# Filter placement by 32-column array tiles, x in half loads, and turns moved ahead of the rounds, in an FFT mixing and FFN kernel

## The chip, the cores and the metric

The kernel runs on one NeuronCore of a Trainium2 chip. The metric is the device time of one execution in microseconds, the median over several runs; times inside the kernel are from one profiled execution, counted from the start of its span (755.9 us).

## The reference

For each of 8 batches, x (3008 x 256) is filtered along the sequence by an FFT, a product with a complex filter and an inverse FFT. The result, as 24064 rows of 256, goes through an FFN with a squared ReLU.

```python
X = np.fft.rfft(x, axis=1)
Y = X * (filt_r + 1j * filt_i)[None, :, :]
y = np.fft.irfft(Y, n=x.shape[1], axis=1)        # 8 x 3008 x 256
h = np.maximum(y.reshape(24064, 256) @ w_in, 0)  # w_in 256 x 2048
out = (h * h) @ w_out                            # w_out 2048 x 256
```

## The kernel before

The length 3008 is split as 64 x 47, and the transforms are matmuls with constant matrices. A batch passes through five stages:

- stage A, 47-point transforms of x; batch 0 has a form of its own (`chunk_a0`, L375 and L377, evicted to `uT` by ScalarE in L384 and VectorE in L386) because it comes first and nothing else can run yet;
- the turn: batch 0's result is transposed on TensorE by an identity (`turn_u`, L394, evicted to `ut` in L400 and L402); later batches go through DRAM;
- stage B (`unit_b`, L417) and the product with the filter on VectorE (L425), which writes `prods`;
- stage P (`unit_p0`, L448), evicted by ScalarE to `ze` (L450), written to DRAM and read back in another layout as `zt`;
- stage Y (`unit_y`, L498), which gives `yt`, the input of the FFN (`ffn_g1`, L528, with the ReLU in L532).

The filter reaches its place by matmuls too. Its 1504 rows are loaded flat on 128 partitions (L237), cast to 16 bits, and moved by `place_f`: for each of 24 channels, a matmul with a 0/1 matrix picks the rows of the lower half (L284), a second one those of the upper half and adds them (L287). Both matrices are 128 x 128 and write all 128 output partitions, because each of 4 groups of 32 partitions holds one of the two halves (`low, up, low, up`). ScalarE evicts the result to `sF` (L295), the imaginary part with a sign by partition. `place_f(im, k)` covers four channels; there are six for the real and six for the imaginary part.

The order is written out by hand, and each engine runs its instructions in that order. Before the planned main loop there is a prologue for batch 0: the three loads of x, 1 MB each (`load_wide`, L215), then the filters and constants on the same queue; 26 warm-up matmuls on zeros (L265); five halves of x cast by VectorE and one by GpSimd (L219); stage A in four chunks; turns 0 to 3; a real placement; the casts of the imaginary filter; turn 4, a real placement, turn 5, an imaginary placement; then seven rounds. A round runs two `unit_b`, an imaginary placement between them, a `unit_p0` of the round before and a real placement. After the rounds come batch 1's stage A (L348), fill matmuls that keep TensorE busy (L799), stage Y of batch 0, and the loop over the FFN, into which the later batches' stages are planned by due times.

PSUM has three kinds of pairs: `psH` (two tiles of two banks), `psF` and `psO` (two of one bank each). `bank_pair` hands them out in turn: psH, psH, the psF pair, the psO pair. In the rounds placements and `unit_p0` share the two psH tiles, so each waits for the eviction of the one before the last.

Of the kernel before, what the change touches and what calls it, by code (L numbers as in the profile page):

```python
# [9 lines left out]
F16 = mybir.dt.float16  # L10
# [10 lines left out]
SLOTS = 8  # L21
CLS = 376
QF = 3008
PQ = ((0, 0), (0, 1), (0, 2), (1, 2), (1, 3), (1, 0))


def _build_consts():
    N = N1 * N2
    n2 = np.arange(N2)
    m = np.arange(NM)  # L30


    SA = np.zeros((N2, 2, 2, 2, NC))
    for c in range(NC):
        for h in range(2):
            SA[:, h, h, 0, c] = np.cos(2 * np.pi * n2 * c / N2)
            SA[:, h, h, 1, c] = np.sin(2 * np.pi * n2 * c / N2)

    S0 = np.zeros((128, 6, 2, 48))
    for h in range(2):
        q = SA[:, h, h].reshape(N2, 48)
        for t in range(2):
            S0[2 * h + t::4, t, h] = q[:32]
        for c in range(4):
            S0[4 * h + c:120:8, 2 + c, h] = q[32:]


    freq = np.full((NC, 64), -1)  # L50
    for c in range(NC):
        for j in range(32):
            freq[c, j] = 47 * j + c
            if c:
                freq[c, 32 + j] = 47 * j + 47 - c
    freq[0, 32] = N // 2


    SB = np.zeros((NM, 2, 2, NC, 2, 64))

    n1j = 8 * (m % 8) + 2 * (m // 8)
    SP = np.zeros((2, 64, NC, 2, 2, NM))
    for c in range(NC):
        for f in range(64):
            k = freq[c, f]
            if k < 0:
                continue
            sg = 1.0 if (f < 32 or c == 0) else -1.0
            for h in range(2):
                th = 2 * np.pi * ((k * (32 * h + m)) % N) / N  # L70
                SB[:, h, 0, c, 0, f] = np.cos(th)
                SB[:, h, 1, c, 0, f] = -sg * np.sin(th)
                SB[:, h, 0, c, 1, f] = -np.sin(th)
                SB[:, h, 1, c, 1, f] = -sg * np.cos(th)
            if c == 0 and f == 32:
                SB[:, :, 1, c, :, f] = 0.0
            w = (1.0 if k in (0, N // 2) else 2.0) / N
            for i in range(2):
                th = 2 * np.pi * ((k * (n1j + i)) % N) / N
                cs, sn = w * np.cos(th), w * np.sin(th)  # L80
                SP[0, f, c, i, 0] = cs
                SP[0, f, c, i, 1] = sg * sn
                SP[1, f, c, i, 0] = -sn
                SP[1, f, c, i, 1] = sg * cs


    SY = np.zeros((32, 2, 2, N2, 2))
    for c in range(NC):
        th = 2 * np.pi * c * n2 / N2
        for i in range(2):  # L90
            SY[c + c // 12 * 4, i, 0, :, i] = np.cos(th)
            SY[c + c // 12 * 4, i, 1, :, i] = -np.sin(th)


    PF = np.zeros((128, 6, 2, 2, 32))
    for w, (s, q) in enumerate(PQ):
        for j in range(32):
            PF[4 * j + q, w, :, s, j] = 1.0

    f16 = lambda a, p: np.ascontiguousarray(a.reshape(p, -1).astype(np.float16))  # L100
    C0 = np.zeros((128, 896))
    C0[:, 0:576] = S0.reshape(128, 6, 2, 2, NC).transpose(0, 1, 4, 2, 3).reshape(128, 576)
    C0[:, 576:704] = np.eye(128)
    for h in range(2):
        C0[64 * h:64 * h + N2, 704:752] = SA[:, h, h].reshape(N2, 48)
    C0[:, 768:862] = SY.reshape(128, 94)
    return f16(C0, 128), f16(PF, 128), f16(SB, 128), f16(SP, 128)


@with_exitstack  # L110
def kernel(
# [90 lines left out]
    sSA = sC1[:, 0:64]  # L202
    sSY = sC1[0:112, 64:158]
    ident = sC0[:, 576:704]
    sPF = p_out.tile([128, 6, 128], F16, tag="ost", name="sPF")

    xw32, xw16 = {}, {}

    def load_wide(k):

        v0 = xrows[0:2048, :].rearrange("(p m) d -> p m d", m=16)
        v1 = xrows[2048:3072, :].rearrange("(p m) d -> p m d", m=8)
        pool, tag = (p_x32, "x32") if k < 2 else (p_h2, "h2")
        t = pool.tile([128, 8, D], F32, tag=tag, name=f"xw_{k}")
        nc.sync.dma_start(out=t, in_=(v0[:, 0:8, :], v1, v0[:, 8:16, :])[k])  # L215
        xw32[k] = t

    def cast(eng, out, in_):
        (eng.copy if eng is nc.scalar else eng.tensor_copy)(out=out, in_=in_)  # L219

    def cast_wide(k, *engs):
        t = p_x16.tile([128, 8, D], F16, tag="x16", name=f"xw16_{k}")
        for i in range(2):
            m = slice(4 * i, 4 * i + 4)
            cast(engs[i], t[:, m, :], xw32[k][:, m, :])
        xw16[k] = t

    for k in range(3):
        load_wide(k)


    f32s = []

# [5 lines left out]
        f32s.append(t)  # L239

    load_f(0)
    nc.sync.dma_start(out=sPF, in_=dPF.ap().rearrange("p (w q) -> p w q", q=128))
    load_f(1)
    nc.sync.dma_start(out=sC1, in_=dC0.ap()[:, 704:896])
    nyq = p_out.tile([128, 2, D], F32, tag="ost", name="nyq")
# [15 lines left out]
    sF = const.tile([128, 2, NC, D], F16, name="sF")  # L261
    nc.vector.memset(sF[:, 0, 0:2, :], 0.0)
    ps = psO("warm").rearrange("p a d -> p (a d)")
    for _ in range(26):
        nc.tensor.matmul(ps, zero, sF[:, 0, 0:2, :], start=True, stop=True)  # L265

    f16s = []
# [1 line left out]
    def place_f(im, k, *engs, rotate=False):  # L269
# [6 lines left out]
        for i in range(4):  # L276
            c = 4 * k + i
            e0, e1 = D * c, D * (47 - c)
            cuts = [0] + [d for d in range(1, D)
                          if (e0 + d) % QF == 0 or (c and (e1 + d) % QF == 0)] + [D]  # L280
            for d0, d1 in zip(cuts, cuts[1:]):
                o = banks[i // 2][:, (i % 2) * D + d0:(i % 2) * D + d1]
                q, a = divmod(e0 + d0, QF)
                nc.tensor.matmul(o, sPF[:, PQ.index((0, q)), :], f16s[0][:, im, a:a + d1 - d0],  # L284
                                 start=True, stop=False)
                q, a = divmod(e1 + d0, QF) if c else (0, QF + d0)
                nc.tensor.matmul(o, sPF[:, PQ.index((1, q)), :], f16s[0][:, im, a:a + d1 - d0],  # L287
                                 start=False, stop=True)
        for t, i in groups:
            n = t.shape[1]  # L290
            eng = engs[i % len(engs)]
# [71 lines left out]
        if b == 1:  # L363
            write_u(b, c)

    def chunk_a0(c):

        for k in range(2):
            banks, groups = bank_pair(f"psA_0_{c}_{k}")
            for dt in range(2):  # L370
                for i in range(4):
                    m = 4 * k + i
                    o = banks[dt][:, 96 * i:96 * i + 96]
                    d = slice(128 * dt, 128 * dt + 128)
                    nc.tensor.matmul(o, xw16[2 * (c % 2)][:, m, d], s0[:, c // 2, :],  # L375
                                     start=True, stop=False)
                    nc.tensor.matmul(o, xw16[1][0:120, m, d], s0[0:120, 2 + c, :],  # L377
                                     start=False, stop=True)
            for dt in range(2):
                m = 32 * c + 16 * k  # L380
                o = uT[:, dt, :, m:m + 16].rearrange("p c (m q) -> p m c q", q=4)
                pv = banks[dt][:, 0:384].rearrange("p (m c q) -> p m c q", m=4, q=4)
                if (pair_engine() is nc.scalar) if len(groups) == 1 else (dt == 0):
                    nc.scalar.copy(out=o, in_=pv)  # L384
                else:
                    nc.vector.tensor_copy(out=o, in_=pv)  # L386

    def turn_u(k, eng):

# [343 lines left out]


    uT = p_h2.tile([128, 2, NC, 128], F16, tag="h2", name="uT")
    for k in range(3):
        cast_wide(k, nc.vector, nc.gpsimd if k == 2 else nc.vector)

    def load_const(t, d, k):
        c = slice(12 * k, 12 * k + 12)  # L740
        nc.sync.dma_start(out=t, in_=d.ap().rearrange("p (a b) -> p a b", b=128)[:, c, :])
# [3 lines left out]
        load_const(sSB[:, c, :], dSB, k)  # L745
        load_const(sSP[:, c, :], dSP, k)
    load_win()
    for c in (0, 2, 1, 3):
        chunk_a0(c)
    f16s.append(p_h2.tile([128, 2, QF + D], F16, tag="h2", name="f16"))  # L750
    e0, e1 = slice(0, 1504), slice(1504, QF)
    for im in range(2):
        nc.gpsimd.tensor_copy(out=f16s[0][:, im, QF:], in_=nyq[:, im, :])
    for e in (e0, e1):
        nc.gpsimd.tensor_copy(out=f16s[0][:, 0, e], in_=f32s[0][:, e])
    uts[0] = p_ut.tile([128, NC, D], F16, tag="ut", name="ut_0")
    turn_u(0, nc.scalar)
    turn_u(1, nc.vector)
    turn_u(2, nc.scalar)
    turn_u(3, nc.vector)  # L760
    place_f(0, 0, nc.scalar, rotate=True)
    for eng, e in ((nc.vector, slice(0, 1024)), (nc.gpsimd, slice(1024, 2048)),
                   (nc.scalar, slice(2048, QF))):
        cast(eng, f16s[0][:, 1, e], f32s[1][:, e])
    turn_u(4, nc.vector)
    place_f(0, 1, nc.scalar, rotate=True)
    turn_u(5, nc.vector)
    place_f(1, 0, nc.scalar, nc.vector, rotate=True)
    for k in range(6):
        if k % 3 == 0:  # L770
# [9 lines left out]
    for k in range(7):  # L780
        if k < 6:
            unit_b(0, 2 * k)
            if k < 5:
                place_f(1, k + 1, nc.scalar)
            unit_b(0, 2 * k + 1)
        if k > 0:
            unit_p0(k - 1)
        if k < 4:
            place_f(0, k + 2, nc.scalar)
    read_z(0, 0)  # L790
    read_z(0, 1)
    tiny = const.tile([1, 1], F16, name="tiny")
# [67 lines left out]
```

## Time and profile before

The median of three runs is 759.61 us (759.55 to 760.27).

| engine | busy us | share of the span |
|---|---|---|
| TensorE matmul | 741.9 | 98% |
| VectorE | 655.4 | 87% |
| ScalarE | 564.2 | 75% |
| GpSimd | 193.9 | 26% |

The change concerns the time before the first FFN matmul, at 50.21 us:

| event | us |
|---|---|
| first cast of x starts | 6.32 |
| stage A, first matmul | 11.23 |
| turns without a further wait from | 17.80 |
| first product with the filter starts | 24.62 |
| last `ze` copy starts | 41.24 |
| stage Y starts | 48.76 |
| first FFN matmul starts | 50.21 |

A row of a timeline gives start, length, engine, line, operation, output and inputs, count, and in brackets how long the engine was idle before and what ended that. Matmul lengths include their latency, so the spacing of starts says more than the length of one. A row of "groups" gives busy time and mean length; idle time there counts only where the engine is the one that the end waits for.

### The profile page before, as it was taken

The page shows a single profiled execution, that of the slowest core. Times are in us where ns is not written, and L with a number is a line of the kernel's source. Part 1 is how long each engine was busy: PE and PEld are TensorE (multiplying, and loading weights), DVE is VectorE, ACT ScalarE, POOL GpSimd, SP SyncE. Part 2 cuts the span into 40 slices and gives each one's busy share as a digit, 9 for nine tenths or more (in the row PEclk, how much of TensorE's full clock was granted, in tenths as well). Part 3 has the DMA queues.
Part 4 walks back from the last instruction along what each step waited for, and adds up shares of the span by engine and source line. Part 5 has one row for each costly group of instructions (what it writes and reads, how often), then busy time and mean ns, then how long its engine had stood idle before and what let it go on. Part 6 is the DMA issues. An engine that isn't in the chain of part 4 may idle for free.

```text
span 755.9 us, 20010 instructions
## 1 busy us (share of the span) xinstructions
PE 741.9 (98%) x8419; PEld 542.8 (72%) x8419; DVE 655.4 (87%) x730; ACT 564.2 (75%) x803; POOL 193.9 (26%) x267
## 2 busy tenths in 40 slices
PE   8988999999999999999999999999999999999998
PEld 5845766777777777877778777787678777777776
DVE  5859998899899898989979998899989989888783
ACT  2967788778878777787777778777777777777773
POOL 3811750244222321232303224033311222000000
PEclk9999999999999999999999999999999999999999
DMA  9994898666785566756586646764547333321011
GB/s 364 298 221 147 144 185 224 174 115 121 165 220 121 97 130 161 194 104 133 107 216 127 131 102 131 229 126 101 115 108 207 80 78 92 99 85 43 30 57 57
DMA packets 103026, 106.51 MB, mean 141 GB/s; under 512 B 10144, under 2 KB 93472, under 8 KB 101400
## 3 DMA queue, kind: packets, MB, share of 16 engines
q1 hardware_dynamic: 83496, 81.99, 35.7%
q0 software_dynamic: 19296, 23.05, 22.1%
q8 instruction: 66, 1.08, 0.6%
q14 instruction: 24, 0.20, 0.1%
q10 hardware_dynamic: 144, 0.18, 0.1%
HBM read 57.97 MB, written 48.23 MB: 141 GB/s over the span
## 4 chain that ended last, share of the span: by engine, by line
PE 90%; DVE 5%; ACT 2%; DMA 1%; issue 1%; ACTq 0%; DVEq 0%
PE psH L528 40%; PE psX L643 21%; PE psY L643 16%; PE psY L498 3%; PE psB L417 2%; PE psP L462 2%; PE psA L348 2%; DVE prod L425 2%; PE warm L265 1%; PE psO L548 1%; ACT h L532 1%; DVE h L539 1%; PE psf L284 1%; PE psf L287 1%; DMA prod<-prod 1%
## 5 line engine op out<-in xcount | busy, mean ns | idle before, releaser
L532 ACT ACTIVATE h<-psH 128x1024 f16<-128x1024 f32 x376 | 385.3, 1026 | 160.2 <-PE psH L528 159.2
L528 PE MATMUL psH<-yt,sWin 128*128 128x512 f16 (+7 forms) x1728 | 386.8, 351 | 1.2 <-ACT h L532 0.4
L539 DVE TENSOR_TENSOR h<-h 128x2048 f16<-128x2048 f16 (+1 forms) x192 | 229.8, 1197 | 45.5 <-ACT h L532 45.1
L432 POOL DMA_DIRECT2D prod<-prod x168 | 138.8, 967 | 428.5 <-DVE prod L425 426.1
L528 PEld LDWEIGHTS <-sWin 128*128 128x128 f16 x1728 | 149.1, 98 | 90.5 <-issue 3.0
L643 PEld LDWEIGHTS <-sum 128*128 128x128 f16 x2944 | 181.4, 98 | 26.2 <-issue 6.3
L643 PEld LDWEIGHTS <-h 128*128 128x128 f16 x2208 | 135.6, 98 | 24.5 <-issue 5.3
L425 DVE TENSOR_TENSOR prod<-psB,sF 128x1024 f16<-128x1024 f32 x84 | 102.3, 1219 | 11.9 <-PE psB L417 11.8
L643 PE MATMUL psX<-sT,sum 128*128 128x128 f16 x1472 | 104.7, 219 | 0.0
L643 PE MATMUL psY<-sT,sum 128*128 128x128 f16 x736 | 71.2, 219 | 0.0
L643 PE MATMUL psY<-sWout,sum 128*128 128x128 f16 x736 | 56.0, 219 | 1.4 <-DVE bot L658 1.4
L617 DVE TENSOR_TENSOR sum<-sum,h 128x2048 f16<-128x2048 f16 x46 | 56.1, 1220 | 0.8
L643 PE MATMUL psY<-sWout,h 128*128 128x128 f16 x736 | 56.2, 219 | 0.0
L643 PE MATMUL psX<-sT,h 128*128 128x128 f16 x736 | 56.1, 219 | 0.0
L620 DVE TENSOR_TENSOR sum<-h 128x2048 f16<-128x2048 f16 x46 | 56.0, 1217 | 0.0
L623 DVE TENSOR_TENSOR sum<-h,sum 128x2048 f16<-128x2048 f16 x46 | 55.9, 1216 | 0.0
L195 POOL DMA_DIRECT2D x<-in_x_dram x64 | 55.8, 1045 | 0.5 <-PE psA L348 0.5
L614 DVE TENSOR_TENSOR sum<-h 128x2048 f16<-128x2048 f16 x46 | 55.9, 1215 | 0.0
L464 ACT CAST ze<-psP 128x512 f16<-128x512 f32 x84 | 49.2, 585 | 1.2 <-PE psP L462 1.1
L643 PE MATMUL psX<-sWout,h 128*128 128x128 f16 x736 | 48.7, 219 | 0.0
L507 DVE CAST yt<-psY 128x376 f16<-128x376 f32 x62 | 33.7, 543 | 14.3 <-PE psY L498 14.1
L498 PE MATMUL psY<-sC,zt 112*128 112x94 f16 x512 | 42.3, 204 | 1.3 <-DMA zt<-dZ 0.9
(78 smaller groups left out, 571.3 us busy)
## 6 DMA issues: line engine op xcount, KB each, us to landing
zt<-dZ SPq DMA_DIRECT2D x64, 192.0 KB
dU<-u SPq DMA_DIRECT2D x56, 192.0 KB
prod<-prod POOLq DMA_DIRECT2D x168, 64.0 KB, 2.7
dZ<-ze SPq DMA_DIRECT2D x28, 384.0 KB
x<-in_x_dram POOLq DMA_DIRECT2D x48, 192.0 KB, 5.3
ut<-dU SPq DMA_DIRECT2D x7, 1024.0 KB
out_dram<-bot SPq DMA_DIRECT2D x32, 128.0 KB
out_dram<-top SPq DMA_DIRECT2D x16, 256.0 KB
```

The costliest lines, as they stand in the source:

```text
L195: nc.gpsimd.dma_start(out=t[64 * h + p0:64 * h + p1], in_=v[p0:p1, 8 * c:8 * c + 8, :])
L425: nc.vector.tensor_mul(out=prod, in0=ps.rearrange("p (a d) -> p a d", d=D).unsqueeze(1).to_broadcast([128, 2, 2, D]), in1=sF[:, :, 2 * p:2 ...
L432: nc.gpsimd.dma_start(out=prod[64 * i:64 * i + 64, 0], in_=prod[64 - 64 * i:128 - 64 * i, 1], accum_op=mybir.AluOpType.add)
L498: nc.tensor.matmul(ps[:, 94 * jj:94 * jj + 94], zt[:, 4 * (g % 2) + jj, dt * 128:(dt + 1) * 128], sSY, start=True, stop=True)
L528: nc.tensor.matmul(ps[:, i, o:o + n], sWin[:, dt, jt * 128:(jt + 1) * 128], yts[b][:, dt, r:r + n], start=(dt == 0), stop=(dt == 1))
L532: nc.scalar.activation(out=h2[:, 2 * s:2 * s + 2, :], in_=ps, func=AF.Relu)
L539: nc.vector.tensor_mul(out=v, in0=v, in1=v)
L614: nc.vector.tensor_add(out=t, in0=a21, in1=a22)
L617: nc.vector.tensor_sub(out=t, in0=f[5], in1=a11)
L620: nc.vector.tensor_sub(out=t, in0=a11, in1=a21)
L623: nc.vector.tensor_sub(out=t, in0=a12, in1=f[6])
L643: nc.tensor.matmul(o[:, t, :], f[p][:, q, 128 * t:128 * t + 128], sg["w"][p][:, q, :], start=(m == 0 and p in (1, 2)), stop=(q == 7), skip ...
```

## The change

It has four parts. The placement matrix becomes four 128 x 32 pieces, and each pair of accumulating 128-wide matmuls becomes four 32-column ones, each writing its own group of 32 output partitions; the array can hold them side by side as four column tiles. The loads of x become six halves of 512 KB in the order in which stage A can use them, with casts, all on VectorE, and stage A's units written in order of arrival; the warm-up shrinks from 26 to 16 matmuls. All six turns come before the placements, turn 4 evicted by ScalarE. Three real placements instead of two come before the rounds, the second evicted by VectorE, and half of the real filter's cast goes from GpSimd to VectorE. It is meant to shorten the way to the first FFN matmul.

```diff
-PQ = ((0, 0), (0, 1), (0, 2), (1, 2), (1, 3), (1, 0))
+WARM = 16
...
-    PF = np.zeros((128, 6, 2, 2, 32))
-    for w, (s, q) in enumerate(PQ):
+    PF = np.zeros((128, 4, 32))
+    for q in range(4):
         for j in range(32):
-            PF[4 * j + q, w, :, s, j] = 1.0
+            PF[4 * j + q, q, j] = 1.0
...
+    def cast_wide(k, i):
+        m = slice(4 * i, 4 * i + 4)
+        nc.vector.tensor_copy(out=xw16[k][:, m, :], in_=xw32[k][:, m, :])
+
+    HALVES = ((0, 0), (1, 0), (0, 1), (1, 1), (2, 0), (2, 1))
+    for k, i in HALVES:
+        load_wide(k, i)
...
-    for _ in range(26):
+    for _ in range(WARM):
...
-                q, a = divmod(e0 + d0, QF)
-                nc.tensor.matmul(o, sPF[:, PQ.index((0, q)), :], f16s[0][:, im, a:a + d1 - d0],
-                                 start=True, stop=False)
-                q, a = divmod(e1 + d0, QF) if c else (0, QF + d0)
-                nc.tensor.matmul(o, sPF[:, PQ.index((1, q)), :], f16s[0][:, im, a:a + d1 - d0],
-                                 start=False, stop=True)
+                low = divmod(e0 + d0, QF)
+                up = divmod(e1 + d0, QF) if c else (0, QF + d0)
+                for r, (q, a) in enumerate((low, up, low, up)):
+                    nc.tensor.matmul(o[32 * r:32 * r + 32, :], sPF[:, q, :],
+                                     f16s[0][:, im, a:a + d1 - d0], start=True, stop=True)
...
-    for k in range(3):
-        cast_wide(k, nc.vector, nc.gpsimd if k == 2 else nc.vector)
...
-    for c in (0, 2, 1, 3):
-        chunk_a0(c)
+    for k, i in HALVES[:2]:
+        cast_wide(k, i)
+    unit_a0(0, 0)
+    unit_a0(2, 0)
+    for k, i in HALVES[2:4]:
+        cast_wide(k, i)
+    unit_a0(0, 1)
+    unit_a0(2, 1)
+    for i in range(2):
+        cast_wide(2, i)
+        unit_a0(1, i)
+        unit_a0(3, i)
...
-    for e in (e0, e1):
-        nc.gpsimd.tensor_copy(out=f16s[0][:, 0, e], in_=f32s[0][:, e])
...
     turn_u(0, nc.scalar)
     turn_u(1, nc.vector)
+    for eng, e in ((nc.gpsimd, slice(0, 1504)), (nc.vector, slice(1504, QF))):
+        cast(eng, f16s[0][:, 0, e], f32s[0][:, e])
     turn_u(2, nc.scalar)
     turn_u(3, nc.vector)
+    turn_u(4, nc.scalar)
+    turn_u(5, nc.vector)
     place_f(0, 0, nc.scalar, rotate=True)
+    place_f(0, 1, nc.vector, rotate=True)
+    place_f(0, 2, nc.scalar, rotate=True)
...
-    turn_u(4, nc.vector)
-    place_f(0, 1, nc.scalar, rotate=True)
-    turn_u(5, nc.vector)
     place_f(1, 0, nc.scalar, nc.vector, rotate=True)
...
-        if k < 4:
-            place_f(0, k + 2, nc.scalar)
+        if k < 3:
+            place_f(0, k + 3, nc.scalar)
```

More of the change, by code (lines that the diff above doesn't have):

```diff
@@ L204, with load_wide @@
     ident = sC0[:, 576:704]
-    sPF = p_out.tile([128, 6, 128], F16, tag="ost", name="sPF")
+    sPF = p_out.tile([128, 4, 32], F16, tag="ost", name="sPF")
     xw32, xw16 = {}, {}
-    def load_wide(k):
+    def load_wide(k, i):
         v0 = xrows[0:2048, :].rearrange("(p m) d -> p m d", m=16)
         v1 = xrows[2048:3072, :].rearrange("(p m) d -> p m d", m=8)
[L213 to L216, printed above, removed]
+        if i == 0:
+            pool, tag = (p_x32, "x32") if k < 2 else (p_h2, "h2")
+            xw32[k] = pool.tile([128, 8, D], F32, tag=tag, name=f"xw_{k}")
+            xw16[k] = p_x16.tile([128, 8, D], F16, tag="x16", name=f"xw16_{k}")
+        m = slice(4 * i, 4 * i + 4)
+        nc.sync.dma_start(out=xw32[k][:, m, :],
+                          in_=(v0[:, 0:8, :], v1, v0[:, 8:16, :])[k][:, m, :])
     def cast(eng, out, in_):
         (eng.copy if eng is nc.scalar else eng.tensor_copy)(out=out, in_=in_)
[L221 to L226, printed above, removed]
-    for k in range(3):
-        load_wide(k)
+    def cast_wide(k, i):
+        m = slice(4 * i, 4 * i + 4)
+        nc.vector.tensor_copy(out=xw16[k][:, m, :], in_=xw32[k][:, m, :])
+    HALVES = ((0, 0), (1, 0), (0, 1), (1, 1), (2, 0), (2, 1))
+    for k, i in HALVES:
+        load_wide(k, i)
     f32s = []
@@ L241 @@
     load_f(0)
-    nc.sync.dma_start(out=sPF, in_=dPF.ap().rearrange("p (w q) -> p w q", q=128))
+    nc.sync.dma_start(out=sPF, in_=dPF.ap().rearrange("p (w q) -> p w q", q=32))
     load_f(1)
@@ L364, in unit_a, with unit_a0 @@
             write_u(b, c)
[L366 to L386, printed above, removed]
+    def unit_a0(c, k):
+        banks, groups = bank_pair(f"psA_0_{c}_{k}")
+        for dt in range(2):
+            for i in range(4):
+                m = 4 * k + i
+                o = banks[dt][:, 96 * i:96 * i + 96]
+                d = slice(128 * dt, 128 * dt + 128)
+                nc.tensor.matmul(o, xw16[2 * (c % 2)][:, m, d], s0[:, c // 2, :],
+                                 start=True, stop=False)
+                nc.tensor.matmul(o, xw16[1][0:120, m, d], s0[0:120, 2 + c, :],
+                                 start=False, stop=True)
+        for dt in range(2):
+            m = 32 * c + 16 * k
+            o = uT[:, dt, :, m:m + 16].rearrange("p c (m q) -> p m c q", q=4)
+            pv = banks[dt][:, 0:384].rearrange("p (m c q) -> p m c q", m=4, q=4)
+            if (pair_engine() is nc.scalar) if len(groups) == 1 else (dt == 0):
+                nc.scalar.copy(out=o, in_=pv)
+            else:
+                nc.vector.tensor_copy(out=o, in_=pv)
     def turn_u(k, eng):
@@ L735 @@
     uT = p_h2.tile([128, 2, NC, 128], F16, tag="h2", name="uT")
-    for k in range(3):
-        cast_wide(k, nc.vector, nc.gpsimd if k == 2 else nc.vector)
     def load_const(t, d, k):
@@ L747 @@
     load_win()
-    for c in (0, 2, 1, 3):
-        chunk_a0(c)
+    for k, i in HALVES[:2]:
[10 more added lines that the diff above has]
+        unit_a0(3, i)
     f16s.append(p_h2.tile([128, 2, QF + D], F16, tag="h2", name="f16"))
-    e0, e1 = slice(0, 1504), slice(1504, QF)
     for im in range(2):
         nc.gpsimd.tensor_copy(out=f16s[0][:, im, QF:], in_=nyq[:, im, :])
-    for e in (e0, e1):
-        nc.gpsimd.tensor_copy(out=f16s[0][:, 0, e], in_=f32s[0][:, e])
     uts[0] = p_ut.tile([128, NC, D], F16, tag="ut", name="ut_0")
```

## The prediction, made before the result was known

> **What bounds the kernel now.** I read the page first: its chain that ended last is TensorE for 90% of the span, and the slices show TensorE at 8 or 9 tenths throughout. All that the diff touches lies before the first FFN matmul (L528, at 50.21 us), so the question is when that matmul starts; what follows is one planned sequence hung on it. Next I read the chain of waits from 0 to 50 us, pieces in order of time (start, length, engine and line):
>
> ```profile
> 2.68 8.72 PE warm L265 x26
> 15.75 2.01 DVE uT L386 x4
> 17.80 1.90 PE psT L394 x31
> ...
> 40.61 0.61 PE psP L448 x4
> 41.24 1.02 ACT ze L450
> 42.28 3.28 DMA dZ<-ze
> 45.58 3.04 DMA zt<-dZ
> ```
>
> The warm-up matmuls hold TensorE to 11.0, then come stage A and its evictions (to 17.75), turns and first placements, the rounds (first product of VectorE 24.62, last `ze` copy ends 42.25), and a trip through DRAM to 48.6. Then the timeline of VectorE alone (start, length, engine, line, operation, idle before and releaser):
>
> ```profile
> 6.32 1.29 DVE L219 CAST xw<-xw 128x1024 f16<-128x1024 f32 x2 [2.67 <-DMA xw<-in_x_dram]
> 8.82 1.29 DVE L219 CAST xw<-xw 128x1024 f16<-128x1024 f32 x2 [1.20 <-DMA xw<-in_x_dram]
> 11.30 0.69 DVE L219 CAST xw<-xw 128x1024 f16<-128x1024 f32 x1 [1.19 <-DMA xw<-in_x_dram]
> 12.87 2.00 DVE L386 CAST uT<-psA 128x384 f16<-128x384 f32 x4 [0.88 <-PE psA L377]
> 15.75 2.00 DVE L386 CAST uT<-psA 128x384 f16<-128x384 f32 x4 [0.88 <-PE psA L377]
> ```
>
> A 1 MB load lands every 2.5 us, and every cast of x is done before the first VectorE eviction. So stage A runs without a gap: 128 matmuls from 11.23 to 16.95, one each 45 ns. The rows of busy time by stretch say what limits each part:
>
> ```profile
> 11.00:17.00 6.00, 6.00 (x130) 5.86 (x128) 3.94 (x8) 3.33 (x8) 4.34 (x5) 1.00 1.01 426
> 24.60:40.60 16.00, 14.80 (x141) 12.58 (x140) 13.95 (x12) 14.48 (x14) 14.49 (x25) 1.00 1.09 248
> ```
>
> (After the length: PE, PEld, DVE, ACT, POOL busy, instructions in brackets, clock, DMA share, GB/s.) Stage A is all TensorE. In the rounds three engines are near full, and ScalarE's evictions follow one another with gaps of 0.1 us (1.02 + 1.11 + 1.01 us in a round of 3.33).
>
> **What the Trainium skill says.** TensorE: Matmul & The Clock Gate, section Architectural detail: ScalarE and VectorE are "strict FIFO", while TensorE can only pull weight loads ahead. The trace agrees where it shows it: VectorE's order is the program's. TensorEngine Tiling (Array Packing), Key Properties: tiles run in parallel, and a change of tiling mode drains the array. The trace agrees: from 41.13, twelve 47x64 matmuls of 512 columns start within 0.46 us, so four run at once (one alone takes 0.216); between the last 128-wide matmul's 0.11 us and the first tile some 0.1 us is lost. Clock Gate page, The HAM clock gate: TensorE starts at half clock and falls back after an idle window of about 3.4 us. The trace shows the start: warm-up matmuls every 0.427 us until 8.63, then 0.216. No gap of that length is in it later.
>
> **The change part by part.**
>
> *Warm-up, 26 to 16.* By the present pace the 15th starts at 8.63 and the 16th at 8.85, so TensorE is free at 9.1. With latency, stage A begins at 9.2, 2.0 us earlier. The halves of x land at about 5.1, 6.3, 7.6, 8.8, 10.1, 11.3 (1.25 us each, half the spacing above); the first two casts (0.69 each) end near 7.0, so the warm-up decides.
>
> *Stage A in order of arrival.* VectorE's program order becomes: two casts, two evictions, two casts, two evictions, a cast, two evictions, a cast, two evictions. Each cast waits for its load only, but behind evictions that wait for TensorE; and the next TensorE group waits for that cast. What ran side by side becomes a ring of four groups. One group is 32 matmuls x 45 ns = 1.44 us, 0.2 to the eviction (before: last start 12.63, eviction 12.87), evictions 0.5 apart (553 ns mean), then casts of 0.69 (1.29 a pair), then 0.2 to the next matmul.
> - Group 1: matmuls 9.2 to 10.6, evictions 10.8 to 11.8, casts to 13.1.
> - Group 2: 13.3 to 14.75, second eviction to 15.5, cast to 16.1.
> - Group 3: 16.3 to 17.75, evictions to 19.0, cast to 19.6.
> - Group 4: 19.8 to 21.25, last eviction to 22.0.
>
> The turns start at 22.05 against 17.80: 2.0 won, 6.3 lost, 4.25 later. ScalarE's half of the evictions (480 ns) hides beside VectorE's. GpSimd's cast of x (1.56) goes, but its filter casts write a buffer freed by VectorE's last cast, so they start near 19.6; with 0.81 + 1.44 + 1.04 they end at 22.9, before they are needed.
>
> *Turns and real placements ahead.* VectorE, in order: turn 1.15, half of the real filter's cast 1.1 (1504 columns; 1024 took 0.86), two half evictions 1.2, turn 1.15, placement 1.2, imaginary cast 0.86: 6.7 us in a row from 23.1 (turns 22.05 + 16 x 56 ns + 0.2), so to 29.8. Only then can the first imaginary placement run, 0.5, and ScalarE's eviction with the sign, 1.1, with 0.35 of latencies: the first product at 31.75. ScalarE's own share (0.9 + 1.1 + 0.9 + 1.1 + 1.0 + 1.0) hides beside it. Before, the step from turns to product was 6.8; it becomes 9.7. First product: 7.1 late.
>
> *Array tiles.* A placement had 8 matmuls of 256 columns at 109 ns = 0.87 us. It gets 16 of 32 columns; four at once gives 4 x 109 = 0.44, with issue 0.5. No 32-column tile is in the trace: if they serialise it is 16 x 109 = 1.75. I take 0.5, since the 64x64 tiles overlap fully here. A mode change costs about 0.1 each way. The saving is worth little: the placements wait for ScalarE to free their PSUM pair, and ScalarE keeps eight of its nine placement evictions in the rounds.
>
> *Rounds.* ScalarE: 5 x 1.11 + 3 x 1.02 + 6 x 1.01 = 14.7 us, less 1.02 than before. VectorE: twelve products at 1.16 = 13.9. Laid out by the alternating PSUM pair, the eleventh product waits for the last imaginary placement (43.3), the last product ends at 45.95, the last `ze` at 47.65. The rounds take 15.9 instead of 17.6 (24.62 to 42.25): 1.7 back. `ze` is 5.4 late.
>
> *Trip through DRAM and on.* 6.3 us before, with the DMA engines full until 45. The output-weight load issued at 34.19, taking 8.9, will have landed by then, so I allow up to 0.7 less. The floor is TensorE's own queue: batch 1's stage A and the fill, 7.6 us from 41.13 to 48.76. I take 5.0 later for the first FFN matmul. All that follows waits for data from here, and its loads are issued relative to it, so the shift reaches the end.
>
> Sum: 4.25 (stage A) + 2.85 (turns to first product) - 1.7 (rounds) - 0.4 (DRAM) = +5.0 us; 759.6 + 5.0 = **764.6**. The smaller DMA of the placement matrix (192 to 32 KB) and two constants less cost nothing: nobody waits for them.
>
> **Rivals.**
> - *As it is meant (7%).* Evictions do not hold the casts back: stage A starts 2.0 earlier and stays gapless, the rounds give 1.7: 759.6 - 3.7 = 755.9. For it: every half of x has landed by 11.3. Against it: a queue in order. If gains and losses cancel (4%): 759.6.
> - *Slower still (13%).* The rests between groups, 2.5, 1.4 and 2.0 us, bring the clock down, and each later group takes 2.9 instead of 1.44: 3 x 1.44 = 4.3 more, 768.9. Or tiles do not overlap: (1.75 - 0.5) x 4 ahead of the rounds, mostly exposed, and 8 x 1.25 in them with TensorE at 12 x 0.22 + 6 x 0.87 + 8 x 1.75 = 21.9: about 6 more there, near 770. For the first: the ring leaves TensorE idle over half of its time. Against: no rest is 3.4 us long, and the tiles overlap at 41.13.
> - *A milder loss (6%).* The clock rises one window earlier and the warm-up ends at 8, or the DRAM trip shrinks by 1.5: 762 to 763.
>
> **How the numbers follow.** The ring as worked out has 70%: 764.6. Slower: 0.70 + 0.13 + 0.06 = 0.89; same 0.04; faster 0.07. The range leaves out the fast cases and the far end of the slow ones: 762.0 (milder loss) to 768.5 (a partly cold stage A).
>
> **What would show it.** Right: VectorE casts of x near 12, 15.5 and 19, each straight after an eviction, with TensorE waiting for VectorE in three gaps between 10.6 and 19.8; turns near 22; first product near 31.7; placements of about 0.5 us; first FFN matmul near 55. Wrong: stage A gapless, matmuls of 96 columns at 90 ns, or placements of 1.7 us. The likeliest error is a shift that the plan swallows between 50 and 90 us, where VectorE and ScalarE set the pace in turn.

## The result, and the profile after

The changed kernel takes 765.02 us (median of 6, 763.86 to 765.47) against 759.58 us (median of 6, 757.33 to 760.27): a ratio of 1.0073, 95% interval 1.0058 to 1.0088, so 5.4 us slower. The forecast was 764.6. The number is close, in part by luck: the working behind it is less good, as the account below shows.

First the chain of waits of the kernel after, 0 to 60 us (start, length, engine and line; counts after x):

```profile
2.68 6.51 PE warm L265 x16
10.66 1.02 DVE uT L384 x2
11.68 1.21 DVE xw L226 x2
14.54 0.56 DVE uT L384
15.10 0.61 DVE xw L226
18.54 1.02 DVE uT L384 x2
19.56 0.61 DVE xw L226
22.99 0.57 DVE uT L384
23.61 1.79 PE psT L392 x15
...
49.56 1.02 ACT ze L448
50.60 2.42 DMA dZ<-ze
53.16 3.43 DMA zt<-dZ
...
58.17 1.18 PE psH L526 x4
```

Where the chain of before went from the warm-up through one stretch of evictions to the turns, it now goes eviction, cast, three times round, and ends with a last eviction. Between them lie the matmuls of stage A, in pieces too short for this list. The warm-up ends at 9.2 as planned, but the turns start at 23.61 (before 17.80) and the first FFN matmul at 58.17 (before 50.21, +7.96). The rest of the span is untouched: 763.7 - 58.2 = 705.5 us against 755.9 - 50.2 = 705.7.

The timeline of VectorE shows the casts of x straight after evictions, with no idle time ahead of them, so no load was waited for; the last cast, at 19.48, is like these:

```profile
10.66 1.02 DVE L384 CAST uT<-psA 128x384 f16<-128x384 f32 x2 [3.44 <-PE psA L375]
11.60 1.28 DVE L226 CAST xw<-xw 128x1024 f16<-128x1024 f32 x2
...
15.02 0.68 DVE L226 CAST xw<-xw 128x1024 f16<-128x1024 f32 x1
```

The list of waits of the same kernel has both sides of the ring, VectorE's evictions behind TensorE and TensorE behind VectorE's casts (total, times, longest):

```profile
DVE uT L384 <- PE psA L375: 9.7, 6, 3.4
PE psA L373 <- DVE xw L226: 4.7, 3, 1.7
```

And the rows of busy time by stretch (after the length: PE, PEld, DVE, ACT, POOL busy, instructions in brackets, then granted clock, DMA share, GB/s):

```profile
15.00:16.50 1.50, 0.74 (x10) 0.75 (x11) 0.70 (x2) 0.00 (x0) 0.00 (x0) 0.62 1.07 445
16.50:18.00 1.50, 1.50 (x23) 1.50 (x21) 0.00 (x0) 0.74 (x2) 0.00 (x0) 0.50 0.95 401
```

Stage A of before had 6.00 us of TensorE in 6.00 at a clock of 1.00. Here TensorE rests, and the third and fourth group run at half clock. By the timeline of TensorE, group 1's 32 matmuls start from 9.02 to 10.42, one per 45 ns; groups 3 and 4 from 15.76 to 18.22 and from 20.22 to 22.68, one per 79 ns. The bulk of group 2 starts at 12.94, after one lone matmul at 12.34, and its last one starts at 14.30. The clock is full again from 26 us and falls once more later: VectorE's work in a row ahead of the rounds leaves TensorE busy for 0.10 us between 30 and 32, and the clock is 0.61 from 32 to 34 and 0.54 from 34 to 36.

### The profile page after: what moved, and what is told of

It is laid out like the page before. It is cut to its first block, busy times and chain, and to the rows that moved or that the text cites. A ratio compares the mean times of both kernels' runs of the same rounds, so it can differ in the third digit from the quotient of the medians.

```text
span 763.7 us, 20209 instructions
## 1 busy us (share of the span) xinstructions
PE 742.6 (97%) x8517; PEld 539.8 (71%) x8517; DVE 656.9 (86%) x732; ACT 563.9 (74%) x803; POOL 191.4 (25%) x265
## 4 chain that ended last, share of the span: by engine, by line
PE 90%; DVE 5%; DMA 2%; ACT 1%; issue 1%; SPq 0%; ACTq 0%; DVEq 0%
PE psH L526 40%; PE psX L641 21%; PE psY L641 16%; PE psB L415 3%; PE psY L496 3%; PE psP L460 2%; PE psA L347 2%; DVE prod L423 1%; PE psO L546 1%; PE warm L265 1%; DVE h L537 1%; DMA dU<-u 1%; PE psf L286 1%; PE psP L446 1%; PE psA L373 1%
## 5 line engine op out<-in xcount | busy, mean ns | idle before, releaser
L496 PE MATMUL psY<-sC,zt 112*128 112x94 f16 x512 | 42.3, 204 | 0.9 <-DMA zt<-dZ 0.5
```

Source lines behind the costliest of these rows:

```text
L496: nc.tensor.matmul(ps[:, 94 * jj:94 * jj + 94], zt[:, 4 * (g % 2) + jj, dt * 128:(dt + 1) * 128], sSY, start=True, stop=True)
```

## Experiments

Each kernel was timed in turn with the unchanged one on the same chip; the medians of that one are 759.06 us (37 runs; e1 to e4), 758.95 (60; e5 to e9) and 759.49 (31; the rest). The ratio is to that kernel, as recorded for these executions; it need not be exactly the quotient of two medians. The four columns of times are read from each profile: first product of VectorE, start of the last `ze` copy, first FFN matmul, and the span. The profiled execution need not be the median one.

| kernel | first product | last ze | FFN starts | span | median us | ratio, 95% interval |
|---|---|---|---|---|---|---|
| before | 24.62 | 41.24 | 50.21 | 755.9 | 759.58 | |
| after | 33.77 | 49.56 | 58.17 | 763.7 | 765.02 | 1.0058 to 1.0088 |
| e1 casts ahead | 25.47 | 41.28 | 51.99 | 758.8 | 759.91 | 0.9995 to 1.0018 |
| e2 rests filled | 30.62 | 46.21 | 54.43 | 760.7 | 762.49 | 1.0030 to 1.0060 |
| e3 tiles only | 23.68 | 39.25 | 49.46 | 756.5 | 759.54 | 0.9993 to 1.0012 |
| e4 turns only | 26.42 | 41.97 | 50.90 | 756.5 | 759.61 | 1.0000 to 1.0018 |
| e5 warm-up only | 24.20 | 40.86 | 50.40 | 757.9 | 759.75 | 0.9999 to 1.0018 |
| e7 late weights | 25.46 | 41.28 | 49.75 | 756.2 | 757.17 | 0.9963 to 0.9984 |
| e8 e7, old turns | 24.57 | 40.14 | 48.58 | 754.3 | 756.80 | 0.9967 to 0.9984 |
| e9 longer fill | 25.35 | 40.81 | 51.14 | 756.6 | 758.79 | 0.9994 to 1.0015 |
| before again | 24.75 | 41.41 | 51.17 | 759.6 | 761.37 (one run) | |
| e10 before, late weights | 24.37 | 41.03 | 49.09 | 756.1 | 758.58 | 0.9980 to 1.0002 |
| e11 after, late weights | 33.10 | 48.54 | 56.97 | 762.9 | 764.64 | 1.0063 to 1.0092 |
| e12 e8, turn first | 24.06 | 39.64 | 48.12 | 753.9 | 756.23 | 0.9954 to 0.9981 |

**e1: the casts ahead of the evictions.** The changed kernel with nothing altered but the order of VectorE's casts and the evictions of stage A. Theory: the ring costs the time. Rival: something else in the change does (tiles, turns, half loads).

```diff
-    for k, i in HALVES[:2]:
+    for k, i in HALVES[:4]:
         cast_wide(k, i)
     unit_a0(0, 0)
+    cast_wide(2, 0)
     unit_a0(2, 0)
-    for k, i in HALVES[2:4]:
-        cast_wide(k, i)
+    cast_wide(2, 1)
     unit_a0(0, 1)
     unit_a0(2, 1)
     for i in range(2):
-        cast_wide(2, i)
         unit_a0(1, i)
```

> The changed kernel with nothing but VectorE's order altered: the casts of x stand ahead of the evictions that wait for TensorE. If the ring of casts behind evictions is the cause (theory), stage A runs nearly gapless from 9.0, the turns start near 15.7 instead of 23.6, the clock stays full, and the time falls by about 8 us against the changed kernel, to about 757, some 2.5 us under the kernel before. If the tiles, or the turns and placements moved ahead, are what costs (rival), the turns come earlier but the first FFN matmul does not, and the time stays near 764.

Stage A hardly rests (TensorE busy for 5.79 us from 9 to 15, first row of its stretches below), the turns start at 15.81 and the first product comes 8.3 us earlier than in the changed kernel. Of these 8.3 us the time keeps 5.1: 759.91 us. So the ring, with the fall of the clock that it brings, carries nearly all of the 5.4 us lost, and the rival falls. But the theory missed by 3 us. The profiles show where: of the 8.3 us at the last `ze` copy, 6.2 are left at the first FFN matmul and 4.9 in the span. The chain of e1:

```profile
42.31 4.57 DMA dZ<-ze
47.02 3.38 DMA zt<-dZ
...
51.99 4.60 PE psH L526 x12
```

and its stretches, with the columns as above:

```profile
9.00:15.00 6.00, 5.79 (x128) 5.62 (x125) 5.04 (x11) 3.64 (x8) 0.74 (x2) 1.00 1.04 429
48.00:50.00 2.00, 0.00 (x0) 0.00 (x0) 0.00 (x0) 0.00 (x0) 0.64 (x1) 1.00 0.98 215
50.00:52.00 2.00, 1.19 (x23) 1.11 (x24) 0.80 (x2) 0.94 (x2) 0.00 (x0) 1.00 1.08 155
52.00:54.00 2.00, 2.00 (x6) 0.69 (x6) 0.30 (x1) 0.23 (x1) 0.00 (x0) 0.61 1.31 210
```

The write of dZ takes 4.57 us where it took 2.42 after the changed kernel's later rounds; TensorE, whose fill is used up, rests from 48 to 50.5, and the first twelve FFN matmuls then run mostly at half clock (0.61 from 52 to 54, 0.53 in the two microseconds after). An earlier end of the rounds is partly spent here.

**e2: the rests filled.** The changed kernel with 9, 5 and 7 matmuls of zeros by 512 columns written into the three rests of the ring. It leaves the ring as it is and is meant to take away only the fall of the clock in stage A.

```diff
+    def fill_a(n):
+        ps = psF("fillA")
+        for _ in range(n):
+            nc.tensor.matmul(ps, zero, sF[:, 0, 0:2, :], start=True, stop=True)
...
+    fill_a(9)
     unit_a0(0, 1)
     unit_a0(2, 1)
...
+    cast_wide(2, 0)
+    fill_a(5)
+    unit_a0(1, 0)
+    unit_a0(3, 0)
+    cast_wide(2, 1)
+    fill_a(7)
+    unit_a0(1, 1)
+    unit_a0(3, 1)
...
```

> The changed kernel with matmuls on zeros (9, 5 and 7 of 512 columns) put on TensorE into the three rests of stage A, each shorter than its rest; nothing else is altered. If the fallen clock is part of the loss, the third and fourth group run at 45 ns a matmul instead of 80 (2.2 us) and the turns at full clock (0.9 us): about 3 us less than the changed kernel, 762. If only the waiting counts and the clock is hidden behind VectorE, it stays at 765.

762.49 us, 2.5 less than the changed kernel, and its row for 19.0 to 21.5 us, with group 4 in it, shows the clock held (the rows before it, from 9 us on, have 1.00 too; the fall ahead of the rounds is still there, 0.64 from 28 to 30 and 0.50 from 30 to 32):

```profile
19.00:21.50 2.50, 2.08 (x40) 1.80 (x39) 1.11 (x2) 0.96 (x2) 2.50 (x4) 1.00 1.02 412
```

Its turns start at 21.12, 2.49 earlier than the 23.61 of the changed kernel; 0.24 of that comes from a warm-up that ended earlier in this execution (8.95 instead of 9.19). The first FFN matmul is 3.7 earlier in the profile. By the medians the fall of the clock in stage A costs 2.5 us, and by the start of the turns 2.3 to 2.5. The waits of the ring cost 21.12 - 15.81 = 5.3 us against e1.

**e3: tiles only, and e4: turns only.** The kernel before with the placement of the change alone (e3), and with its new order of turns and placements alone (e4).

```diff
-                q, a = divmod(e0 + d0, QF)
-                nc.tensor.matmul(o, sPF[:, PQ.index((0, q)), :], ...
...
+                for r, (q, a) in enumerate((low, up, low, up)):
+                    nc.tensor.matmul(o[32 * r:32 * r + 32, :], sPF[:, q, :], ...
...
```

> The kernel before with only the placement by four 32-column tiles. Theory: a placement takes 0.5 us of TensorE instead of 0.87, hidden behind ScalarE's evictions in the rounds; ahead of them TensorE is the limit and three placements save up to 1.1 us: 758.5 to 759.6. Rival (tiles cost by mode changes and weight loads): slower than before by 1 us or more.

The last `ze` copy starts at 39.25 instead of 41.24, so the tiles do shorten the rounds by about 1 us, and the first product comes about 1 us earlier too. The time is the same, 759.54 us. The chain of e3 shows why:

```profile
40.29 4.42 DMA dZ<-ze
44.73 3.15 DMA zt<-dZ
```

The trip through DRAM takes 7.6 us instead of 6.3. Of 2 us gained, the first FFN matmul keeps 0.75, and the median nothing that can be told.

```diff
     turn_u(0, nc.scalar)
     turn_u(1, nc.vector)
+    for eng, e in ((nc.gpsimd, slice(0, 1504)), (nc.vector, slice(1504, QF))):
+        cast(eng, f16s[0][:, 0, e], f32s[0][:, e])
     turn_u(2, nc.scalar)
     turn_u(3, nc.vector)
+    turn_u(4, nc.scalar)
+    turn_u(5, nc.vector)
     place_f(0, 0, nc.scalar, rotate=True)
+    place_f(0, 1, nc.vector, rotate=True)
+    place_f(0, 2, nc.scalar, rotate=True)
...
```

> The kernel before with only the turns and real placements moved ahead of the rounds (with their engines and the split cast of the real filter), placements still by 128-wide matmuls. Theory: the step from turns to the first product grows from 6.8 to about 10 us, the rounds shrink by 1.7: about 1.5 us slower than before, 761. Rival (the move pays as it is meant): 1 us or more faster than before.

In e4 turns to first product takes 26.42 - 16.44 = 9.98 us, against 6.8 before. The rounds win 1.1 us of these 3.2 back (16.6 instead of 17.6), and the warm-up of this execution ended 1.4 earlier than in the profile of before, so its last `ze` copy starts only 0.7 later. The median is 759.61 us, 0.55 above its kernel before, with an interval that touches no change: the 1.5 us expected are not there. The step is real in the trace and worth at most 0.2% in the time.

**e5: the shorter warm-up only.**

```diff
-    for _ in range(26):
+    for _ in range(16):
```

> The kernel before with 16 warm-up matmuls in place of 26, nothing else: part 1 of the change alone. Theory: TensorE is free at 9.1 instead of 11.2, but with whole 1 MB loads the second cast pair ends near 10.1, so stage A begins at about 10.3, 0.9 earlier; that moves the turns and the rounds by 0.9 and, as the shortened DRAM trip of the other runs does not pass such gains on, the time by 0 to -0.5: 759.0 to 759.6. Rival (the shorter warm-up is what lets the clock fall): matmuls of stage A at 80 ns, turns 1 us or more later, over 761.

759.75 us, no change that can be told, and the clock of stage A stays full (1.00 in its stretches from 9 to 17 us), so the rival falls. What stops most of the gain is in the timeline of VectorE in e5:

```profile
20.35 1.51 DVE L219 CAST f<-f 128x1024 f16<-128x1024 f32 x1 [0.61 <-DMA f<-in_filt_i_dram]
```

The turns start 1.5 us earlier (16.27), but VectorE's cast of the imaginary filter then waits 0.61 us for its load, which the chain of e5 has landing at 20.22. So 0.4 us is left at the first product and at the last `ze` copy, and the trip, 6.9 us instead of 6.3, takes that. Behind the warm-up stand the loads: first those of x, then that of the imaginary filter.

**e7: the output weights out of the way.** e1 has half of the output weights loading from 35.05 on, just ahead of the write of dZ. e7 is e1 with that load moved behind the first reads of dZ.

```diff
-    load_wout(0)
     cast_win()
...
     nc.gpsimd.tensor_copy(out=tiny, in_=ztiles[0][0:1, 0, 0:1])
+    load_wout(0)
     load_wout(1)
```

> The kernel e1 (changed kernel with the casts of x ahead of the evictions), with the first half of the output weights loaded after the first three reads of dZ, beside the second half, and not ahead of the rounds. If that load is what stretches the trip through DRAM in e1 (write 4.57, read 3.38 us): write near 2.5 us, first FFN matmul near 49.5 at full clock, and 755 to 756.5 us. If the trip is stretched by the loads of the second batch's x alone, or the time hangs on something after it: write over 4 us and 759.5 us as e1; if the weights then come too late, a wait of the second FFN product near 61 us and over 760.

757.17 us, 2.7 less than e1, though the rounds end at the same moment. Its chain:

```profile
42.32 2.37 DMA dZ<-ze
44.82 3.34 DMA zt<-dZ
```

The write is back at 2.37 us, and the first FFN matmul starts at 49.75 at full clock. So it was this load, and not those of the second batch's x, that stretched the write. What it did to the earlier writes is in the DMA queues (packets, MB, share of 16 engines) from 38.0 to 42.3, while two earlier writes of dZ are under way and the last one is about to be issued. First e1:

```profile
q0 software_dynamic: 906, 0.46, 85.1%
q1 hardware_dynamic: 874, 0.44, 34.9%
```

then e7:

```profile
q1 hardware_dynamic: 1374, 0.68, 52.6%
...
q0 software_dynamic: 2, 0.00, 0.5%
```

In e1 the weights (GpSimd's queue, q0) hold the engines, and the writes (SyncE's, q1) move 0.44 MB in the time in which they move 0.68 in e7. From 42.3 to 44.5 only 0.02 MB of the weights are left in e1, but SyncE's queue moves 0.56 MB, more than the 256 KB of the last write: it finds the earlier ones not done. The Trainium skill, in DMA: Bandwidth & Descriptors, section Issuing engines are not separate DMA queues, says that transfers started by any engine run on the same 16 DMA engines and interleave; this case agrees, with 0.46 and 0.44 MB moved side by side in those 4.3 us. The time came out 0.7 us above the upper end of what the theory gave.

**e8: e7 with the old order of turns.** Part 4 undone; tiles, halves and the short warm-up stay.

```diff
     turn_u(3, nc.vector)
-    turn_u(4, nc.scalar)
-    turn_u(5, nc.vector)
     place_f(0, 0, nc.scalar, rotate=True)
-    place_f(0, 1, nc.vector, rotate=True)
-    place_f(0, 2, nc.scalar, rotate=True)
...
+    turn_u(4, nc.vector)
+    place_f(0, 1, nc.scalar, rotate=True)
+    turn_u(5, nc.vector)
...
```

> The kernel e7 with the turns and placements in the order of the kernel before (part 4 undone): array tiles, half loads and 16 warm-up matmuls stay. The step from turns to first product goes back from 9.7 to about 7, so the first product comes near 22.8 instead of 25.5; the rounds take 1 us more. By the theory that the start of the FFN follows from the sum: last ze near 39.5, first FFN matmul 1 to 1.5 us before that of e7, limited by batch 1's stage A on TensorE (7.6 us from the end of the rounds): 754 to 756 us. Rival (gains ahead of the DRAM trip are eaten by it): the trip grows by what the rounds win, and the time is that of e7 within 0.5.

The first product comes at 24.57, not 22.8: VectorE's cast of the imaginary filter waits 1.38 us for its load, as in e5. The first FFN matmul is 1.2 us ahead of e7's; the median, 756.80 us, is above the expected range and can't be told from e7's.

**e9: a longer fill.** e1 with 24 fill matmuls instead of 13.

```diff
-    for _ in range(13):
+    for _ in range(24):
```

> The kernel e1 with 24 fill matmuls instead of 13 between batch 1's stage A and the products that wait for the DRAM trip, 2.4 us more at 0.22 us each. In e1 TensorE rests 2.6 us there, and the first FFN matmuls run at half clock. If that rest costs the clock: no half-clock stretch after 50 us, and 757 to 758.5 us. If the clock at the FFN's start is worth nothing, 759.9 us as e1.

The clock is full after 50 us in its stretches, so in e1 it is the rest that lowers it:

```profile
50.00:52.00 2.00, 1.72 (x23) 1.11 (x21) 1.10 (x2) 0.94 (x2) 0.00 (x0) 1.00 1.19 183
```

The median is 758.79 us, above the expected range, and its ratio (1.0005) can't be told from e1's (1.0006), although its profiled span is 2.2 us shorter. Inconclusive as to the time. In its chain the fill itself, which ends near 49.7, is the last thing that the FFN waits for, so part of what the clock gave may have gone into waiting for the fill; how much is not shown.

**Before, a second profile.**

> The kernel before, unchanged, for a second profile. Its first profile has a span of 755.9 us, and the execution timed beside it is at the low end of the kernel's times (757.3 to 762.5, median 759). If the spread lies in the trip through DRAM and what follows at the FFN's start, this profile shows a first FFN matmul other than 50.2 us by as much as its span differs from 755.9; if it lies in the passes, the first FFN matmul is at 50.2 within 0.3 and the rest of the span differs from 705.7.

This execution took 761.37 us, 3.7 more than the one first profiled (757.66), and the spans differ by the same 3.7. Its chain and stretches:

```profile
42.44 4.04 DMA dZ<-ze
46.50 3.08 DMA zt<-dZ
```

```profile
50.00:52.00 2.00, 1.72 (x23) 1.07 (x20) 1.10 (x2) 0.94 (x2) 0.00 (x0) 0.79 1.21 191
52.00:54.00 2.00, 2.00 (x6) 0.73 (x5) 0.00 (x0) 0.93 (x1) 0.00 (x0) 0.50 1.31 214
```

Up to the last `ze` copy it is within 0.2 us of the first profile. Then the write takes 4.04 us instead of 3.28, TensorE rests (busy for 0.35 us between 48 and 50), and the FFN starts 0.96 late at half clock. Neither way of the expectation holds as it stands: 0.96 of the 3.7 us lie before the first FFN matmul and 2.7 after it, the half-clock stretch among them. The kernel before pays in some executions what e1 pays; the profile that I predicted from happened to be one that did not.

**e10 and e11: the late load in the two original kernels.** The edit of e7, in the kernel before and in the changed one.

> The kernel before, with only the first half of the output weights loaded after the first reads of dZ. Its trip through DRAM is 3.28 + 3.04 us, against 2.37 + 3.34 in the kernel e7. If the gain of e7 over e1 is the freed trip, before can win about 0.9 of it: write near 2.4, first FFN matmul 0.5 to 0.9 earlier, 758.1 to 758.6 us. Then most of e7's 1.8 us comes from the earlier rounds and not from the load. If the load alone makes the gain: 757.2 us.

> The changed kernel, with only the same load moved. Its rounds end at 50.6 us, when that load has landed anyway, and its trip is short already (2.42 + 3.43 us). Theory: nothing to win, 764.6 to 765.4 us, or worse if the weights then come too late. Rival (the load stretches the trip whenever the rounds end): 762.5 to 763.5.

Before goes to 758.58 us, within what was expected, 0.9 less (the interval just reaches no change, so the gain is not clear of noise). In its profile the first FFN matmul starts 1.1 us earlier, and the fill ends last ahead of it, not the trip. The changed kernel stays at 764.64: its rounds end when the load has landed anyway. So the load costs e1, whose rounds end near 42 us, while the changed kernel is free of it because it is late. Of e7's gain over before (1.8 us), the load in before would account for about half. The other half is not explained by earlier rounds, as I had expected: e7's last `ze` copy starts at 41.28, that of before at 41.24. e10's executions still spread from 756.9 to 763.0 us; what makes the long ones long stays open.

**e12: a turn ahead of the cast that waits.** e8 with VectorE's fifth turn before the cast of the imaginary filter.

```diff
+    turn_u(4, nc.vector)
     for eng, e in ((nc.vector, slice(0, 1024)), (nc.gpsimd, slice(1024, 2048)),
                    (nc.scalar, slice(2048, QF))):
         cast(eng, f16s[0][:, 1, e], f32s[1][:, e])
-    turn_u(4, nc.vector)
```

> The kernel e8 with VectorE's turn of the fifth column pair ahead of its cast of the imaginary filter: in e8 that cast waits 1.38 us for the filter's load, with two turns queued behind it. Theory: the turn fills the wait, first product 1.0 to 1.3 us earlier than e8's, last ze near 39; the first FFN matmul follows by 0.5 to 1, since batch 1's stage A on TensorE moves along: 755.8 to 756.3 us. Rival (from here on the trip or TensorE's queue sets the FFN's start): 756.8 us as e8.

VectorE of e12:

```profile
19.59 1.23 DVE L400 CAST ut<-psT 128x1024 f16<-128x1024 f32 x1 [0.41 <-PE psT L392]
20.73 1.40 DVE L222 CAST f<-f 128x1024 f16<-128x1024 f32 x1
...
24.06 6.88 DVE L423 TENSOR_TENSOR prods<-psB,sF 128x1024 f16<-128x1024 f32 x6 [0.74 <-PE psB L415]
```

The wait is filled, but the first product comes only 0.5 earlier than in e8, where 1.0 to 1.3 was expected, since VectorE now waits 0.74 for TensorE's product. 756.23 us is the lowest median of all, 0.33% below the kernel before; its interval overlaps those of e7 and e8.

## Why the prediction was right, and where its working was not

**The ring: right.** The group starts were forecast at 9.2, 13.3, 16.3 and 19.8; they are 9.02, 12.94, 15.76 and 20.22. The fourth came that near by luck: the third group ran at half clock, and in e2, at full clock, the later starts are 12.71, 15.53 and 18.86, each a little earlier than forecast. Casts follow evictions, TensorE waits three times for VectorE, and e1 shows that undoing the order alone gives 5.1 of the 5.4 us back.

**Stage A, 4.25 us later: it was 5.81 (23.61 - 17.80).** Two sizes were off, in opposite directions. The waits of the ring cost 5.3 us by e2 and e1, not 6.3. But I set aside the fall of the clock with "no rest is 3.4 us long", and that step failed: rests of 2.5 and 1.5 us, from last to first matmul of neighbouring groups, were enough to bring it to half as the third group began, it stayed there over the next rest of 2.0 us, and e2 puts the cost at about 2.5 us. The rival that had it charged all three later groups, 4.3 us; only the third and fourth ran at half clock, at 79 instead of 45 ns. That is near the 90 ns that the prediction named as a sign of being wrong. The Trainium skill has a passage that I should have weighed: TensorE: Matmul & The Clock Gate, section A second HAM failure mode: psum-queue depth-cycling, tells of a kernel whose short idle times between groups of matmuls made the clock oscillate. This trace agrees with it, at a clock of 0.50 after rests of 2.5 and 1.5 us, and does not bear out the idle window of about 3.4 us as a safe bound.

**Turns to first product, 9.7 us: 10.16** (33.77 - 23.61). The term fits at full clock: it is 9.66 in e1 and 9.62 in e7, whose turns run at 1.00. In the changed kernel VectorE's work in a row takes 6.4 us (25.43 to 31.84; 6.7 was laid out), but it begins later, 1.8 after the turns start instead of 1.05: the clock is still at half there, and the chain has 1.79 us for 15 matmuls of a turn that take 1.03 in e7.

**Rounds, 15.9 us: 16.8** (33.77 to 50.58). The term was mis-sized by 0.9. The late start is not the reason: in e1 the rounds start 8.3 us earlier and take 16.8 too. But the prediction put nothing for the clock here either. With the turns ahead and the tiles, TensorE rests for 2.1 us before the rounds, in e1 as in the changed kernel, and the first placements of the rounds run at half clock, as this stretch of e1 shows:

```profile
25.00:28.00 3.00, 3.00 (x49) 1.40 (x46) 2.53 (x3) 2.40 (x3) 2.87 (x7) 0.52 1.09 378
```

Where the half-clock stretch ends sooner after the first product, the rounds are shorter: 16.5 us in e9 and e11, 16.6 in e2. So some 0.3 us of the 0.9 may be the clock's. No run has the new order and the tiles at full clock, so how the rest divides stays open.

**Placements: right in size, wrong in what they save.** At full clock a placement in the rounds takes 0.55 to 0.62 us, where 16 matmuls one after the other, at the 109 ns of one of 256 columns, would take 1.75, so the tiles do overlap. At half clock it takes 0.97. That ScalarE would hide the saving is not what e3 shows: with the tiles alone the first product comes 0.9 us earlier, and the rounds take 16.6 instead of 17.6. What e3 wins goes into the trip.

**Trip through DRAM, 0.4 shorter: right,** 6.0 against 6.4 us from the end of `ze` to the landing of zt, and for the reason given: the output weights have landed, and the write takes 2.42 instead of 3.28 us. That it is this load is what e7 and e11 show.

**The sum.** The terms measured are 5.81 + 3.34 - 0.82 - 0.35 = +7.98 us, and the first FFN matmul moved by 7.96. The sum forecast was +5.0. Three of the prediction's own signs of being right were missed with it: turns near 22 (23.61), first product near 31.7 (33.77), first FFN matmul near 55 (58.17). That the time still came out at 765.02 is due to the other end: I added a shift read from one profile to a median. The profiled execution of before took 757.66, 1.92 below its median, and that of after 765.47, 0.45 above its own: 7.81 - 1.92 - 0.45 = 5.44.

The second profile of before shows one thing that a longer execution can hold, a stretched trip and a half-clock start of the FFN, which the changed kernel escapes. By the recorded clocks it is at most a small part of what the median holds. Over the 128 executions of the unchanged kernel recorded with e1 to e12, 40 have a mean granted clock of 0.998 or less, as the second profile has, and their median is 760.09 us. The other 88 have 0.999 or 1.000 and a median of 758.67, still 1.0 above the execution that I predicted from. What that 1.0 is stays open.

So the sign, the ring and the trip were right, and the fall of the clock, some 2.5 us in stage A and more after it, was missing. An execution of before that was 1.9 us below its median hid most of that. That the forecast lies 0.4 us from the measured time is luck.

**As it is meant: it could have been.** The rival in which stage A stays gapless was e1's 759.91, not 755.9: a gain ahead of the trip is spent in it. With the casts ahead and the weights moved as well, e7, e8 and e12 take 756.2 to 757.2 us.

## What to carry to other kernels

When several engines share one stage, write the order of each in-order queue down and look for a ring. Here casts whose data had landed stood behind evictions that waited for another engine, and undoing this one order was worth 5.1 us, while all four parts of the change together, without the ring, gave nothing that can be told (e1 against before). In e8 it is the other way round: there a cast that waited for its load stood ahead of turns that were ready. A gain in front of a DRAM round trip has to be followed through it: ask which loads the earlier write now meets, and what TensorE does meanwhile. And before adding a shift from a profile to a median, compare the profiled execution with the median.

## What the runs showed of the hardware that I had not expected

- TensorE's granted clock fell to half between bursts of 1.4 us with rests of 2.5 us (one lone matmul in it) and 1.5 us (0.62 in the stretch from 15.0 to 16.5), and stayed there through a gapless burst (0.50 from 16.5 to 18). Zero matmuls in the rests held it at 1.00 (e2, 9.0 to 21.5 us).
- In e1 a rest of 2.6 us ahead of the FFN was enough, with TensorE busy for 1.19 of the 2.00 us after it. The fall came in the stretch 1.5 us and more after the rest had ended (1.00 from 50 to 52, 0.61 from 52 to 54). A rest of 2.1 us ahead of the rounds, which ended at 23.6, was followed by 0.52 from 25 to 28. In e4 a rest of 1.85 us at that place was not followed by a fall.
- A 256 KB write of dZ took 4.57 instead of 2.37 us after 512 KB of weights that another engine had issued 7 us earlier, although only 0.02 MB of that load was moved after the write was issued: the loss is handed on by the writes in between, which moved 0.44 instead of 0.68 MB in the 4.3 us before it.
